# Narrower zero matmuls, masks and selections on GpSimd, and earlier value turns in a fused Sinkhorn attention and maxout kernel

## Chip, cores and metric

The kernel runs on one core of one Trainium2 chip. The metric is the device time of one execution in microseconds (us). In the profile, PE is TensorE's matrix multiplication, PEld its weight load, DVE is VectorE, ACT is ScalarE, POOL is GpSimd and SP is SyncE.

## The reference

Block-sorted attention comes first, and a two-branch maxout layer reads its output. There are 4 batches of 8 heads, 768 positions and head size 64. A sequence has 8 blocks of 96 positions. A small matrix per head (`sort_net`, 8 by 8) goes through five rounds of exponential and of row and column normalisation (Sinkhorn); the result mixes whole blocks of keys and of values. Then each query block attends to its own mixed block.

```python
P = sort_net
for _ in range(5):
    P = P - np.max(P, axis=-1, keepdims=True)
    P = np.exp(P)
    P = P / (np.sum(P, axis=-1, keepdims=True) + 1e-09)
    P = P / (np.sum(P, axis=-2, keepdims=True) + 1e-09)
k_sorted = np.einsum('bhij,bhjcd->bhicd', P, k_b)      # blocks of keys mixed
v_sorted = np.einsum('bhij,bhjcd->bhicd', P, v_b)      # blocks of values mixed
scores = scale * np.matmul(q_b, k_sb.transpose(0, 1, 2, 4, 3))
attn = softmax(scores)                                 # written out in the original
x = np.matmul(attn, v_sb)                              # to 3072 tokens x 512
g = np.maximum(x @ w1, x @ w2)                         # 512 -> 1024
out = g @ w_out                                        # 1024 -> 512
```

Inputs and output are float32; the kernel computes its large products in bfloat16.

## The kernel before

The order of the instructions on each engine is written out by hand (a manual schedule). There are four PSUM buffers of one tag, `ps`, which all TensorE work takes in turn, so a product may have to wait until an earlier one has been copied out. The copies go to ScalarE ("A") or VectorE ("D"), by a letter in the list of steps or by a running count of load (`pick`).

**The opening.** TensorE first runs zero matmuls (`keep_streaming`, with the tile `fill`), 86 of 142 columns, and 12 more of 512 columns: six behind each of two memsets of late weights (`late_zeros`) that stand in rounds 3 and 4 of `sinkhorn`. Meanwhile VectorE and ScalarE run the five rounds of `sinkhorn` on a 32 by 64 tile. In between, `masks` builds `id64`, `maskM` and `maskJ` on VectorE, `selections(0)` builds two selection tiles for batch 0 on VectorE, and ScalarE turns the raw values of batch 0 (`turn_v`, a copy that changes the layout) in four pieces. The last result of the rounds is `p_bf`.

`block_diagonals_first` then expands `p_bf` on TensorE with the constant tiles `one_j` and `sel_v[0]`, and VectorE makes from it the diagonal `bd_k[0]` for the keys, and then `bd_v[0]` for the values. VectorE turns the last piece of the values. Behind it stand two copies that repeat columns of `maskJ` for the later batches; `block_diagonals` (step `pe2`) reads them much later.

**GpSimd** issues the input DMAs, in this order: values of batch 0 (three pieces), keys (three), queries (four). Behind them it builds the selection tiles of batches 1 to 3 (seven copies) and `one_j` (a memset and a copy), and then issues the weights: four DMAs of 256 columns and two of 512 for `w1` and `w2`, then two for `w_out`. Two subtractions (`w_difference`) and the keys of batch 1 follow. A DMA takes the same semaphore as the eighth before it, and waits for that one.

**The front** is a list of steps for batch 0, which begins

```python
front = """
    k0D k1A k2D v1D v2A v3A tq0D v0A tq1D SC1 SC0 F1
    SC2 VA1 SC5 VA0 SC3 F2 VA2 SC4 F0 tx0D SC6 VA3 ...
```

`k` is a third of the key sort with its copy, `v` a quarter of the value sort, `tq` query transposes, `SC` scores with their exponential on ScalarE, `VA` the product with the values and the normalisation on VectorE (a reciprocal and a multiplication), `tx` the transposes of the result, `h` the maxout layer's first product. `k0` begins with zero matmuls, 1024 columns in two of 512. An `F` asks for 512 columns of zeros ahead of the next step.

**The tails.** After the front, each batch's maxout layer is cut into units, and the steps of the next batch's attention stand behind numbered units: `first_tail`, `second_tail`, `third_tail`. `TURN` is `turn_v` on both halves of the values on VectorE, in four pieces of 24 columns. In `second_tail` the pieces stand behind units 8, 9, 11 and 12; the value sorts that read them (`VS`) stand behind 14 and 16. The keys and queries of batch 3 are loaded into the buffer of the raw values, and so behind the turns.

## Time and profile before

| | us |
|---|---|
| median of 4 runs | 167.45 |
| lowest and highest | 167.06 and 167.72 |
| the profiled execution, its own time | 167.49 |
| its span in the profile | 165.7 |
| PE busy in it | 157.9 |
| ACT, DVE, POOL busy | 83.3, 76.5, 32.3 |

The span runs from the first to the last instruction of the program; the rest of the execution's own time lies around it. A row of the timeline has the start, the length, the engine, the line, the operation with output and inputs, and in brackets how long the engine had been idle and what ended that. A row of the chain has start, length and engine. Records of neighbouring instructions of one engine may overlap, since an instruction starts while the one before it is still finishing.

### The profile page before, as it was taken

How to read it: one execution, taken by the hardware profiler on the slowest of the kernel's cores; microseconds unless marked ns; L12 is line 12 of the kernel's file. 1: busy time of each engine (PE TensorE's matmuls, PEld its weight loads, DVE VectorE, ACT ScalarE, POOL GpSimd, SP SyncE). 2: the span in 40 equal slices, each digit the busy share in tenths (PEclk: the TensorE clock that was granted, in tenths of full speed). 3: DMA queues.
4: the chain of work that ended last, by engine and by line, in shares of the span. 5: the costliest groups of instructions: out<-in, count | busy, mean ns of one | idle time of the engine just before them, and what ended most of it. 6: DMA issues, size and time to landing. Idle time of an engine off the chain costs nothing.

```text
span 165.7 us, 4544 instructions
## 1 busy us (share of the span) xinstructions
PE 157.9 (95%) x2000; PEld 96.3 (58%) x2018; DVE 76.5 (46%) x173; ACT 83.3 (50%) x102; POOL 32.3 (19%) x55
## 2 busy tenths in 40 slices
PE   7999899999999999999899999999999999999992
PEld 7948678656555555557555554575655446554451
DVE  4879779465474564615257874250642420000011
ACT  3585985927149845066552253467446306642020
POOL 7998586232013000000004020000000000000000
PEclk9999999999999999999999999999999999999999
DMA  3999999999999996689503999996025294000333
GB/s 51 198 205 197 198 208 205 211 204 223 209 202 213 218 247 70 186 109 188 112 0 62 169 214 179 240 248 39 0 51 174 49 163 142 0 0 0 127 128 129
DMA packets 30404, 23.90 MB, mean 144 GB/s; under 512 B 16752, under 2 KB 25200, under 8 KB 30384
## 3 DMA queue, kind: packets, MB, share of 16 engines
q0 software_dynamic: 11040, 13.37, 47.9%
q1 hardware_dynamic: 19200, 10.17, 28.5%
q8 instruction: 16, 0.26, 0.6%
q10 hardware_dynamic: 144, 0.07, 0.1%
q14 instruction: 4, 0.03, 0.1%
HBM read 26.75 MB, written 6.29 MB: 199 GB/s over the span
## 4 chain that ended last, share of the span: by engine, by line
PE 78%; DVE 9%; DMA 5%; issue 4%; ACT 2%; ACTq 0%
PE out_ps L715 33%; PE h_ps L688 23%; PE o_ps L586 4%; PE wc_ps L668 4%; DMA qT<-q_pair 4%; PE s_ps L559 4%; PE k_ps L469 2%; PE tq_ps L444 2%; ACT e L567 1%; DVE v_dc L257 1%; PE v_ps L534 1%; PE tw_ps L649 1%; PE v_ps L490 1%; DMA p_sb<-in_sort_net_dram 1%; PE tx_ps L624 1%
## 5 line engine op out<-in xcount | busy, mean ns | idle before, releaser
L715 PE MATMUL out_ps<-wo_sb,g 128*128 128x512 bf16 (+2 forms) x187 | 46.0, 370 | 1.4 <-issue 1.0
L688 PE MATMUL h_ps<-xT,w_sb 128*128 128x384 bf16 x256 | 44.5, 326 | 0.0
L688 PEld LDWEIGHTS <-w_sb 128*128 128x128 bf16 x256 | 24.0, 98 | 15.6
L567 ACT ACTIVATE e<-s_ps 96x768 bf16<-96x768 f32 x32 | 23.9, 804 | 13.7 <-PE s_ps L559 13.5
L702 ACT ACTIVATE g<-h_ps 128x768 bf16<-128x768 f32 x27 | 21.8, 811 | 17.8 <-PE h_ps L688 17.7
L715 PEld LDWEIGHTS <-g 128*128 128x128 bf16 x200 | 17.1, 97 | 15.8
L715 PE MATMUL out_ps<-wc,xT 128*128 128x512 bf16 (+2 forms) x98 | 24.7, 370 | 0.1
L108 ACT COPY o<-out_ps 128x1024 f32<-128x1024 f32 x10 | 10.1, 1012 | 28.3 <-PE out_ps L715 25.6
L603 DVE TENSOR_TENSOR x<-o_ps,rs 96x512 bf16<-96x512 f32 x32 | 22.0, 687 | 1.1
L715 PEld LDWEIGHTS <-xT 128*128 128x128 bf16 x100 | 9.6, 97 | 11.2
L586 PEld LDWEIGHTS <-e 96*128 96x128 bf16 x256 | 11.8, 97 | 5.9 <-DVE v_sb L110 0.2
L597 DVE RECIPROCAL rs<-o_ps 96x8 f32<-96x8 f32 x32 | 6.4, 201 | 18.1 <-PE o_ps L586 17.9
L750 DVE COPY o<-out_ps 128x512 f32<-128x512 f32 (+1 forms) x2 | 1.2, 624 | 27.6 <-PE out_ps L715 27.6
L586 PE MATMUL o_ps<-v_sb,e 96*128 96x65 bf16 x256 | 12.9, 193 | 0.0
L110 DVE CAST kT<-k_ps 128x1024 bf16<-128x1024 f32 x7 | 8.3, 1215 | 7.2 <-PE k_ps L469 7.2
L108 ACT CAST v_sb<-v_ps 96x1024 bf16<-96x1024 f32 x10 | 9.8, 1014 | 2.5 <-PE v_ps L490 0.9
L704 DVE TENSOR_SCALAR g<-h_ps 128x768 bf16<-128x768 f32 x5 | 4.8, 956 | 12.2 <-PE h_ps L688 12.2
L559 PE MATMUL s_ps<-qT,kT 64*128 64x96 bf16 x256 | 8.6, 204 | 1.3 <-DMA qT<-q_pair 0.6
L160 POOL DMA_DIRECT2D v_raw<-in_k_dram x3 | 2.5, 823 | 36.8 <-DVE rs L597 36.7
L559 PEld LDWEIGHTS <-kT 64*128 64x128 bf16 x256 | 6.1, 94 | 6.1 <-issue 3.2
L110 DVE CAST v_sb<-v_ps 96x1024 bf16<-96x1024 f32 x6 | 7.3, 1216 | 4.5 <-PE v_ps L534 2.2
L169 POOL DMA_DIRECT2D v_raw<-in_v_dram x11 | 5.9, 543 | 14.4 <-DVE v_dc L257 9.0
(96 smaller groups left out, 144.9 us busy)
## 6 DMA issues: line engine op xcount, KB each, us to landing
out_dram<-o SPq DMA_DIRECT2D x11, 512.0 KB, 3.2
v_raw<-in_v_dram POOLq DMA_DIRECT2D x8, 384.0 KB, 12.4
k_raw<-in_k_dram POOLq DMA_DIRECT2D x9, 256.0 KB, 10.0
w_sb<-in_moe_w_dram POOLq DMA_DIRECT2D x4, 256.0 KB, 7.8
w_sb<-in_moe_w_dram POOLq DMA_DIRECT2D x2, 512.0 KB, 10.9
wo_sb<-in_moe_w_out_dram POOLq DMA_DIRECT2D x2, 512.0 KB, 14.6
v_raw<-in_v_dram POOLq DMA_DIRECT2D x3, 256.0 KB, 4.7
q_raw<-in_q_dram POOLq DMA_DIRECT2D x4, 192.0 KB, 8.7
```

Source lines behind the costliest of these rows:

```text
L108: nc.scalar.copy(out=out_ap, in_=in_ap)
L110: nc.vector.tensor_copy(out=out_ap, in_=in_ap)
L169: nc.gpsimd.dma_start(out=v_raw[r0 : r0 + 64, m * n : (m + 1) * n], in_=v_src[b, :, m * n : (m + 1) * n],)
L559: nc.tensor.matmul(ps[:, h2 * 512 + ii * 128 : h2 * 512 + ii * 128 + BLK], kT[b][rows, (hp * 8 + i) * BLK : (hp * 8 + i) * BLK + 128], rhs ...
L567: nc.scalar.activation(out=e[:, 0 : 8 * BLK].rearrange("p (t c r) -> p t c r", t=8, r=R), in_=ps[0:BLK] .rearrange("p (t f) -> p t f", t=8 ...
L586: nc.tensor.matmul(ps[:, h2 * 512 + ii * 65 : h2 * 512 + (ii + 1) * 65], e[:, (h2 * 4 + ii) * BLK : (h2 * 4 + ii) * BLK + 128], v_sb[:, m0 ...
L597: nc.vector.reciprocal(out=rs, in_=ov[:, :, :, 64])
L603: nc.vector.tensor_tensor(out=x, in0=ov[:, :, :, 0:D], in1=rs.to_broadcast([BLK, 2, 4, D]), op=ALU.mult,)
L668: nc.tensor.matmul(ps[:, 0:512], w2T[:, fb, dmt * 128 : (dmt + 1) * 128], wo_sb[:, fb, :], start=(fb == 0), stop=(fb == NFB - 1),)
L688: nc.tensor.matmul(h_ps[ch, t][:, m * 512 : m * 512 + TCH], w1_sb[:, hp, fb * 128 : (fb + 1) * 128], xT[:, b % 2, ch, hp % 2, hp // 2, :], ...
L702: nc.scalar.activation(out=g, in_=src, func=AF.Relu)
L715: nc.tensor.matmul(dst, g_tiles[b, ch, m // 2][:, m % 2, off : off + 128] if m < NFB else xT[:, b % 2, ch, hp % 2, hp // 2, off : off + 12 ...
```

## The change

The zero matmuls of the opening have 126 columns and not 142, and the two ahead of the first key sort 320 and not 512. The selections of batch 0 and the two copies of `maskJ` are made by GpSimd. In GpSimd's program, `one_j` comes first behind the queries, its memset written as 32-bit words; then the selections of batch 0, the copies of `maskJ`, four weight DMAs, the selections of batches 1 to 3, and the remaining weight DMAs, the subtractions and the keys of batch 1 in the old order. In `second_tail` the four turns stand behind units 6, 8, 9 and 11. The allocations of `id64`, `maskJ` and `maskM` move up in the text. The order of instructions on TensorE, ScalarE and SyncE is the same; VectorE's changes by the four removed copies and by the places of the turns: the first turn comes ahead of one `g` copy of the maxout layer.

```diff
-    for b in range(1, B):
-        selections(b)
     one_j = const.tile([G, 8 * 130], BF16, tag="one_j", name="one_j")
-    nc.gpsimd.memset(one_j, 0.0)
+    nc.gpsimd.memset(one_j.bitcast(U32), 0)
     nc.gpsimd.tensor_copy(
...
-    for t in range(2):
-        load_w_columns(w2_sb, moe_w2, t, t + 1)
-        load_w_columns(w1_sb, moe_w1, t, t + 1)
-    load_w_columns(w2_sb, moe_w2, 2, 4)
-    load_w_columns(w1_sb, moe_w1, 2, 4)
-    load_w(wo_sb, moe_w_out)
+    selections(0)
...
-    w_difference(0, nc.gpsimd)
-    w_difference(1, nc.gpsimd)
-    load_k(1)
...
-        keep_streaming(ps, n)
+        keep_streaming(ps, n, most=320)
...
-    keep_streaming(ps_f32("fill_ps"), 86 * 142, most=142)
+    keep_streaming(ps_f32("fill_ps"), 86 * 126, most=126)
     for it in range(5):
         sinkhorn(it)
         if it < 3:
             masks(it)
         if it == 2:
-            selections(0, nc.vector)
             turn_v(first, "A", 0, 18)
         if it == 3:
             turn_v(first, "A", 18, 36)
+    for c, n, m in [(2, 2, 0), (4, 3, 1)]:
+        nc.gpsimd.tensor_copy(
+            out=maskJ[:, c : c + n],
+            in_=maskJ[:, m].to_broadcast([128, NB, n]).transpose([0, 2, 1]),
+        )
+    for t in range(2):
+        load_w_columns(w2_sb, moe_w2, t, t + 1)
+        load_w_columns(w1_sb, moe_w1, t, t + 1)
+    for b in range(1, B):
+        selections(b)
+    load_w_columns(w2_sb, moe_w2, 2, 4)
+    load_w_columns(w1_sb, moe_w1, 2, 4)
+    load_w(wo_sb, moe_w_out)
+    w_difference(0, nc.gpsimd)
+    w_difference(1, nc.gpsimd)
+    load_k(1)
...
-            sort_k(0, n[0], 1024 if step == front[0] else 0, eng)
+            sort_k(0, n[0], 640 if step == front[0] else 0, eng)
...
-    for c, n, m in [(2, 2, 0), (4, 3, 1)]:
-        nc.vector.tensor_copy(
-            out=maskJ[:, c : c + n],
-            in_=maskJ[:, m].to_broadcast([128, NB, n]).transpose([0, 2, 1]),
-        )
...
-        6: SC[2:4],
+        6: SC[2:4] + [TURN[0]],
         7: [VA[1], TR[0]],
-        8: [VA[2], TURN[0]],
-        9: [VA[3], TR[1], TURN[1]],
+        8: [VA[2], TURN[1]],
+        9: [VA[3], TR[1], TURN[2]],
         10: SC[4:7],
-        11: [VA[4], TURN[2]],
-        12: [VA[5], TR[2], TURN[3], lambda: load_k(3), lambda: load_q(3)],
+        11: [VA[4], TURN[3]],
+        12: [VA[5], TR[2], lambda: load_k(3), lambda: load_q(3)],
```

## The prediction

> **What bounds the kernel now.** I read the page first, then the chain of waits over the whole span, then the timeline of the opening (0 to 25 us), engine by engine, and of the stretch from 78 to 104 us, where the turns are.

> ```profile
> PE 157.9 (95%) x2000; PEld 96.3 (58%) x2018; DVE 76.5 (46%) x173; ACT 83.3 (50%) x102; POOL 32.3 (19%) x55
> ```

> TensorE is busy 95% of 165.7 us, but before 11.3 us that is zeros. So only two things are worth time: the opening, where a serial VectorE chain is waited for, and holes in TensorE's stream later. Of the larger holes behind 19 us (from the start of each matmul to the next, less its columns), one lies where the diff works: 0.41 us at 96.7. Others are 0.46 at 18.4, 0.62 at 19.6 and 0.72 at 78.9.

> The chain in the opening:

> ```profile
> 11.05 0.23 DVE p_bf L285
> 11.32 0.35 PE pe L367 x8
> ...
> 12.62 0.56 DVE v_dc L257
> 13.18 0.43 DVE maskJ L824 x2
> 13.61 0.88 DVE kT L110
> 14.53 1.09 PE v_ps L490 x32
> ...
> 18.07 0.97 DVE qT L110
> 19.08 0.35 PE s_ps L559 x8
> ```

> The five Sinkhorn rounds end in p_bf, TensorE expands it, VectorE makes the diagonals, turns values, copies the masks and empties the first key sort. The value sorts wait for that buffer, and the first scores for the second query transposes. The starts and lengths of the same stretch are in VectorE's timeline:

> ```profile
> 12.54 0.64 DVE L257 COPY v_dc<-v_raw 64x512 uint32<-64x512 uint32 x1
> 13.11 0.49 DVE L824 COPY maskJ<-maskJ 128x16 f32<-128x16 f32 x2
> 13.27 1.20 DVE L110 CAST kT<-k_ps 128x1024 bf16<-128x1024 f32 x1
> ```

> The chain books 0.43 us on the mask copies, because their records end late (13.60). But the key copy starts at 13.27, while they are open, and takes 1.20 us like the next one (14.40, 1.20). What they hold up is start to start: 13.27 - 13.11 = 0.16.

> **The change, part by part.**

> *Selections of batch 0 off VectorE* (two copies, starts 7.79 and 7.89).

> ```profile
> 7.79 0.28 DVE L204 COPY sel_v<-ident 32x64 bf16<-32x64 bf16 x2
> 8.03 0.11 DVE L87 MEMSET late<- 128x64 uint32 x1
> 8.07 0.15 DVE L278 TENSOR_REDUCE rowsum<-p_sb 32x8 f32<-32x64 f32 x1
> ```

> Their 0.24 us looks serial, but the row sum needs ScalarE's exponential, which runs 7.71 to 7.97. In the next round the row sum starts 0.03 behind it (9.79 to 9.83) and takes 0.21. So without the copies it runs 8.00 to 8.21, in place of 8.07 to 8.22: a gain of 0.01. I take 0. The exponential hides these copies.

> *Opening zeros, 86 x 126 columns.* The row of 86 runs 1.20 to 8.58. Starts are 119 ns apart up to 5.2 us and 62 ns after. With 126 columns I estimate 107 ns and 55 ns, from the columns and from L649, whose 128-column transposes go 16 in 0.89 us (56 ns each). So 37 of the wider-spaced ones up to 5.2, then 49 x 0.055 = 2.7, and 0.2 for the last to finish: end near 8.1, 0.5 earlier. The 12 late zero matmuls (0.216 each) follow; the second six wait for a memset at 9.47 behind the fourth round, so they end about 11.0. But TensorE already idles for p_bf (0.15 before 11.32). Worth 0 here; up to 0.5 in an execution whose fast spacing comes later, where the zeros would end after p_bf. Not below 0.

> *Shorter fill at the first key sort.* Two zero matmuls of 512 become 320: 384 columns at 512 in 0.216, 0.16. The first key matmul moves from 12.18 to 12.02; its diagonal ends at 11.97, plus the 0.05 that p_bf to TensorE takes (11.27 to 11.32): it is ready at 12.02 too. ScalarE's copy of the second key sort (13.42, behind TensorE) moves by 0.16.

> *Masks off VectorE*: 0.16 by starts, 0.43 by the chain's ends. I take 0.16. These two edits serve parallel branches (copies on VectorE, matmuls and ScalarE), so together they are 0.16, not 0.32. After them the second value sort waits for the key copy's end, 14.31 in place of 14.47; transposes, their copies (19.03 to 18.87) and ScalarE's eight exponentials, which run without a break from 18.34 to 24.52, follow. The cover for keeping it is DMA slack: GpSimd's weight differences end at 21.16 and 23.81, first read at 23.54 and 25.72, 1.9 us to spare; the values of batches 1 and 2 land by 46.99 and the turn that reads the last of them runs after 48.1.

> *GpSimd's queue.* Before, behind the query issues: seven copies 7.91 to 9.38, a memset of 1.02 to the next start, one copy, then weights from 10.64. After: memset with half the elements (0.5 to 1.0), a copy (0.24), two selections (0.35), two mask copies (0.2 to 0.35 each by the selection rows), so the first weight DMA is issued at 9.4 to 10.2. Four issues at 0.73; the fourth waits for the last key piece (landed 11.64). Then the seven moved copies, 1.47 in all as before, put the fifth weight issue at 13.9 to 14.6, before 14.14. Two more weight issues, two of the output weights, two differences, and the DMAs of the next keys stand behind that. Landings go in order, 17.56, 18.90, 20.27, 21.56, 24.10, with about 10 us between the fifth issue and its landing; that backlog hides the shift, so 0. Without it, up to 0.5 of lateness, inside the 1.9 spare. The first diagonals need the selections by 11.5, and the masks are read at 35.6.

> *GpSimd beside VectorE.* At 9.24 the multiply took 0.26, its peers 0.21, with a GpSimd copy open: 0.05. Copies stay in the rounds, fewer, but now also run from about 12.4, where the diagonal multiply and the turn are. Net 0; bounds from -0.05 to one copy's length, 0.35 lost. [...]

> *Turns one step sooner* (third batch's tail).

> ```profile
> 95.42 0.83 DVE L257 COPY v_dc<-v_raw 128x768 uint32<-128x768 uint32 x1
> 96.17 0.20 DVE L597 RECIPROCAL rs<-o_ps 96x8 f32<-96x8 f32 x1
> 96.40 0.69 DVE L603 TENSOR_TENSOR x<-o_ps,rs 96x512 bf16<-96x512 f32 x1
> ...
> 97.14 0.41 PE L511 MATMUL v_ps<-bd,v_dc 64*128 64x64 bf16 x16 [0.25 <-DVE x L603]
> ```

> The second value sort waits for a buffer freed by a normalisation at 97.08, queued behind the last turn; the matmul before it starts at 96.70 and its like follow each other by 0.03, so 0.41 is lost. That turn moves to 93.83, the others up likewise, and the first goes into a hole, 1.68 us idle before 85.23 for a turn of 0.83. Then the reciprocal starts at 95.42 and the multiply ends near 96.34, before TensorE gets there (96.73): the whole 0.41 goes, with 0.4 to spare, and next late is nothing but TensorE, whose work fills the chain to 162.7. If the hole were closed, the MoE copy at 85.23 would be late by up to 0.83. The key and query loads that wait for the turns go earlier, the first key piece by about 4.5 us, the query by 1.6; they can slow transposes landing at 89.92 and 95.10, first read near 105. The last query transpose pair lands at 111.52 for scores at 114.60. So 0.41, bounds 0 and 0.45.

> Sum: 0.16 + 0.41 = 0.57. The profiled execution took 167.49 (span 165.7): 166.92. The median of 4 is 167.45, so 166.9.

> **The rivals.** *One of the two is given back*, the early 0.16 to GpSimd copies or the late 0.41 to a new wait: 167.04 to 167.29, no change by the bound of 0.3% (0.50 us, about what a measurement of this kernel can tell from none). For it: 0.16 is small beside 0.35. Against: the stretch after 97 is TensorE alone. *More than the sum*: 0.43 at the masks, and late-clock executions lose up to 0.5 less: 166.35 to 166.6. For it: the chain's ends. Against: two key copies of equal length. *Slower*: shorter zeros leave TensorE idle about 0.3 us near 9.4 and 0.3 before 11.3, and matmul spacing doubles again (the page's clock row reads 9 even in the opening; the spacing tells). At the opening the doubled spacing lasted 4.0 us (1.2 to 5.2), in which 2.0 us of work is done, so +2.0 - 0.41 = 169.0. It decides if holes of 0.3 to 0.4 suffice. Against: holes of 0.46 and 0.62 at 18.4 and 19.6 left the spacing unchanged.

> **How the numbers follow.** Forecast 0.46, more 0.10, one given back 0.34, slower 0.10. Range: low 166.35 from the second rival; high 167.5, both gains lost; the clock case is left out. The forecast's own range is 166.7 to 167.05, a little of it above 166.95, so faster 0.53, same 0.37, slower 0.10.

> **What would show it.** Key copy starting near 13.1, first key matmul at 12.0, scores that start at 19.08 near 18.9; p_bf unmoved within 0.05; TensorE idle longer before it; a turn near 83.5 and no hole between the first two value sorts near 96. Wrong: the multiply at 12.4 longer than 0.3, spacing above 62 ns after 9 us, a MoE copy late at 85, or the early shift gone by 25 us.

## The result and the profile after

| | before | after |
|---|---|---|
| median, us | 167.29 (73 runs) | 166.69 (47 runs) |
| profiled execution, us | 167.49 | 166.42 |
| its span, us | 165.7 | 164.6 |

The ratio is 0.9963, with a 95% interval of 0.9951 to 0.9975: 0.62 us faster (0.42 to 0.82). Disturbed executions are left out of the ratio. The profiled pair differs by 1.07, more than the medians; what is known of the extra 0.45 is told below.

The page's first line after:

```profile
PE 157.4 (96%) x2000; PEld 96.1 (58%) x2018; DVE 76.3 (46%) x169; ACT 83.1 (50%) x102; POOL 32.7 (20%) x59
```

VectorE has four instructions fewer and GpSimd four more. The chain of waits in the opening of the kernel after (start, length, engine and line):

```profile
10.86 0.22 DVE p_bf L278
11.08 0.04 issue
11.12 0.35 PE pe L356 x8
...
17.67 0.97 DVE qT L110
18.64 0.04 issue
18.68 0.35 PE s_ps L548 x8
19.03 0.36 PE o_ps L575 x8
19.39 0.83 issue
20.22 0.34 PE s_ps L548 x8
```

Against before, `p_bf`'s expansion is 0.20 sooner (11.32 to 11.12), and the scores that start behind the second query transposes are 0.40 sooner (19.08 to 18.68). Then comes 0.83 of "issue", a wait that no other engine's work ends. The mask copies are gone from VectorE's timeline, and the turn is followed by the key copies at once:

```profile
12.34 0.61 DVE L250 COPY v_dc<-v_raw 64x512 uint32<-64x512 uint32 x1
12.87 2.34 DVE L110 CAST kT<-k_ps 128x1024 bf16<-128x1024 f32 x2
```

The key copy starts 0.40 sooner (13.27 to 12.87). So by 19 us the opening had brought more than the 0.16 that was forecast. One row later, in TensorE's timeline (in brackets the idle time and what ended it), first of after and then of before, it is gone:

```profile
20.22 0.20 PEld L548 LDWEIGHTS <-kT 64*128 64x128 bf16 x8 [0.96 <-issue]
20.22 0.34 PE L548 MATMUL s_ps<-qT,kT 64*128 64x96 bf16 x8 [0.84 <-PE o_ps L575]
```

```profile
20.23 0.20 PEld L559 LDWEIGHTS <-kT 64*128 64x128 bf16 x8 [0.57 <-issue]
20.23 0.34 PE L559 MATMUL s_ps<-qT,kT 64*128 64x96 bf16 x8 [0.45 <-PE o_ps L586]
```

The step SC5 starts at the same time in both, whatever went ahead of it. From there to 79 us the two executions run 0.01 apart. The 1.07 is gained in two places behind. One is the second value sort, where the forecast put it:

```profile
94.77 0.19 DVE L586 RECIPROCAL rs<-o_ps 96x8 f32<-96x8 f32 x1
95.00 0.69 DVE L592 TENSOR_TENSOR x<-o_ps,rs 96x512 bf16<-96x512 f32 x1
95.68 0.34 PE L548 MATMUL s_ps<-qT,kT 64*128 64x96 bf16 x8
95.86 0.63 PE L500 MATMUL v_ps<-bd,v_dc 64*128 64x64 bf16 x32
```

Both sorts now stand in one row of 32 matmuls in 0.63 us; before, the second 16 waited until 97.14 for the normalisation, which now ends at 95.69, ahead of TensorE. That is 0.42. The other is at 79 us, the first scores of batch 2. Before, then after:

```profile
79.80 0.52 PE L559 MATMUL s_ps<-qT,kT 64*128 64x96 bf16 x16 [0.56 <-DMA qT<-q_pair]
```

```profile
79.17 0.51 PE L548 MATMUL s_ps<-qT,kT 64*128 64x96 bf16 x16
```

The query transpose landed 0.89 sooner and a hole of 0.72 is closed: 0.63 more. Between the opening and 79 us the change alters no instruction: the first turn that it moves starts at 82.83, behind this hole.

### The profile page after: what moved, and what is told of

It is laid out like the page before. It is cut to its first block, busy times and chain, and to the rows that moved or that the text cites. A ratio compares the mean times of both kernels' runs of the same rounds, so it can differ in the third digit from the quotient of the medians.

```text
span 164.6 us, 4545 instructions
## 1 busy us (share of the span) xinstructions
PE 157.4 (96%) x2000; PEld 96.1 (58%) x2018; DVE 76.3 (46%) x169; ACT 83.1 (50%) x102; POOL 32.7 (20%) x59
## 4 chain that ended last, share of the span: by engine, by line
PE 88%; DVE 5%; issue 2%; ACT 2%; DMA 1%
PE out_ps L704 37%; PE h_ps L677 26%; PE o_ps L575 5%; PE wc_ps L657 4%; PE k_ps L458 4%; PE s_ps L548 4%; PE tq_ps L433 2%; PE v_ps L479 1%; PE v_ps L523 1%; PE tw_ps L638 1%; ACT e L556 1%; DMA p_sb<-in_sort_net_dram 1%; PE tx_ps L613 1%; DVE colsum L276 1%; DVE p_sb L273 1%
## 5 line engine op out<-in xcount | busy, mean ns | idle before, releaser
L575 PEld LDWEIGHTS <-e 96*128 96x128 bf16 x256 | 11.7, 97 | 5.9 <-DVE v_sb L110 0.2
L110 DVE CAST kT<-k_ps 128x1024 bf16<-128x1024 f32 x7 | 8.3, 1217 | 9.6 <-PE k_ps L458 9.6
L110 DVE CAST v_sb<-v_ps 96x1024 bf16<-96x1024 f32 x6 | 7.3, 1219 | 5.2 <-PE v_ps L523 2.2
## 6 DMA issues: line engine op xcount, KB each, us to landing
wo_sb<-in_moe_w_out_dram POOLq DMA_DIRECT2D x2, 512.0 KB, 14.5
```

The source lines that it names most:

```text
L110: nc.vector.tensor_copy(out=out_ap, in_=in_ap)
L575: nc.tensor.matmul(ps[:, h2 * 512 + ii * 65 : h2 * 512 + (ii + 1) * 65], e[:, (h2 * 4 + ii) * BLK : (h2 * 4 + ii) * BLK + 128], v_sb[:, m0 ...
```

## Experiments

Each is compared with the kernel before in the same runs. The first four: one half of the change each, and the opening's zeros cut in other ways.

**Turns alone**: the kernel before with the four moved turns and nothing else.

```diff
-        6: SC[2:4],
+        6: SC[2:4] + [TURN[0]],
...
-        8: [VA[2], TURN[0]],
-        9: [VA[3], TR[1], TURN[1]],
+        8: [VA[2], TURN[1]],
+        9: [VA[3], TR[1], TURN[2]],
...
-        11: [VA[4], TURN[2]],
-        12: [VA[5], TR[2], TURN[3], lambda: load_k(3), lambda: load_q(3)],
+        11: [VA[4], TURN[3]],
+        12: [VA[5], TR[2], lambda: load_k(3), lambda: load_q(3)],
```

> The kernel before with only the turns of the third batch moved (units 6, 8, 9, 11). Theory: the hole between the first two value sorts near 97 (0.41 us from start to start) is gone and nothing else moves: 0.42 us less, ratio 0.9975. Rival, that the late gain comes from elsewhere in the change: ratio 1.000, hole still there.

Measured: 166.70, ratio 0.9961 (0.9942 to 0.9980), as much as the whole change. TensorE's timeline in it:

```profile
20.51 0.34 PE L559 MATMUL s_ps<-qT,kT 64*128 64x96 bf16 x8 [0.25 <-PE o_ps L586]
```

```profile
79.45 0.52 PE L559 MATMUL s_ps<-qT,kT 64*128 64x96 bf16 x16
```

```profile
96.15 0.63 PE L511 MATMUL v_ps<-bd,v_dc 64*128 64x64 bf16 x32
```

SC5 is even 0.28 later than before, the value sorts have no hole (0.42 gained), and neither have the scores at 79 (0.63 gained).

**Opening alone**: the changed kernel with the turns back in their old places (the same diff, reversed).

> All of the change but the turns. Theory: in both profiles the fifth score step (SC5) starts at 20.22 to 20.23, though all ahead of it is 0.40 us sooner in the changed kernel, so what the opening gains is swallowed there: ratio 1.000 (within 0.001), SC5 again near 20.2, hole near 97 as before. Rival, the prediction's step: the early 0.16 arrives at the end, ratio 0.9990 or, with what the trace shows, 0.9976.

Measured: 167.10, ratio 0.9982 (0.9964 to 1.0000). SC5 starts at 20.24, the scores at 79 wait again (0.64) and so does the second value sort (0.43). A gain of the opening is not told apart from none here, and neither of the two expected ratios is excluded; in the trace none is left at 20.2.

**Half as many zeros of double width** (43 of 252 columns in place of 86 of 126):

```diff
-    keep_streaming(ps_f32("fill_ps"), 86 * 126, most=126)
+    keep_streaming(ps_f32("fill_ps"), 43 * 252, most=252)
```

> The changed kernel, but the opening zeros are 43 matmuls of 252 columns in place of 86 of 126: 86 fewer TensorE instructions ahead of SC5, the same columns. Theory: SC5 waits for the next 16 KB of TensorE's own instructions (packets of kind instruction, at 11.72, 17.74 and 23.84 in the trace, some 250 instructions each), so the end of the stretch that is already there comes 86 instructions later; SC5 starts near 19.4, and up to 0.8 us is kept at the end: ratio to before 0.991 to 0.995. Rival, a wait for data of the kernel: SC5 stays at 20.2, ratio 0.9963 as the changed kernel.

**Late zeros in four times as many pieces** (128 columns in place of 512):

```diff
-            keep_streaming(ps_f32("fill_ps"), 3072, it)
+            keep_streaming(ps_f32("fill_ps"), 3072, it, most=128)
```

> The changed kernel, but the 12 late zero matmuls of 512 columns become 48 of 128: 72 more TensorE instructions ahead of SC5, the same columns, in a stretch where TensorE idles anyway. Theory (instructions arrive late): TensorE runs dry 72 instructions sooner, in the query transposes or first scores near 17, and resumes near 20; 0.5 to 2.5 us longer than the changed kernel. Rival, a wait for data at SC5: within 0.1 us of the changed kernel, SC5 at 20.2.

Measured: 170.53, ratio 1.0213 (1.0175 to 1.0251), and 171.32, ratio 1.0244 (1.0219 to 1.0269). The same zeros cut otherwise cost 3.1 and 3.9 us against the kernel before, 3.8 and 4.6 against the changed one. For 43 zeros both expectations missed: a gain was forecast, or no change. For the small pieces the direction was right, but 0.5 to 2.5 us had been forecast. TensorE's timeline with 43 zeros, and its table of stretches (busy time of PE, PEld, DVE, ACT and POOL with the number of instructions, then PE's granted clock, the DMA share and GB/s):

```profile
18.42 0.85 PE L433 MATMUL tq_ps<-ident,q_raw 128*64 128x128 bf16 x12 [2.41 <-issue]
```

```profile
15.00:20.00 5.00, 2.55 (x52) 2.05 (x47) 2.10 (x3) 1.79 (x2) 3.68 (x5) 0.68 1.45 197
20.00:25.00 5.00, 4.88 (x87) 3.56 (x85) 2.26 (x6) 3.88 (x6) 4.43 (x5) 0.64 1.27 207
```

The clock fell to 0.68 in the 5 us that hold the hole and was 0.64 in the next 5. In stretches of half a microsecond (PE alone) the fall stands inside the hole, which begins at 16.0 (it is 1.00 up to 16.5):

```profile
16.50:17.00 0.50, 0.00 (x0) 0.81 1.41 188
17.00:17.50 0.50, 0.00 (x0) 0.50 1.47 193
```

It stays at 0.50 up to 23.5. TensorE's timeline with the late zeros in small pieces:

```profile
14.13 0.47 PE L458 MATMUL k_ps<-bd,k_raw 64*64 64x64 bf16 x18 [0.81 <-issue]
...
20.43 0.30 PE L433 MATMUL tq_ps<-ident,q_raw 128*64 128x128 bf16 x3 [2.07 <-issue]
```

Holes that "issue" ends again, elsewhere in the program. Counted over the recorded weight loads and matmuls together, they fall at two places: behind number 445 with 43 zeros, behind 447 and 702 with the small pieces, and behind 701 in before, after and the opening alone. The count is of records, and some are missing (the page of after has 2000 matmuls to 2018 weight loads); the expectations call the two places 448 and 704, an estimate of the author's, and so does the table below. In the one run with both holes they are 255 recorded ones apart (447 to 702), some 256 if a record is missing between them. The page of after shows what may come in such portions:

```profile
q8 instruction: 16, 0.26, 0.6%
```

This queue moves 16 packets of 16,384 bytes, and 15 in the kernel with 43 zeros, which has 43 zero matmuls fewer, each with its weight load. That one packet brings TensorE some 256 instructions, what lies between the two places, is an estimate from these numbers; no record names what a packet holds. The first of the 16 starts at 11.72, when TensorE has been at work since 1.2; how the instructions ahead of number 448 came, the trace doesn't show. From the packet records (starts) and TensorE's timeline:

| kernel | packet's start | TensorE goes on | later by |
|---|---|---|---|
| before, behind 704 | 17.74 | 20.23 | 2.49 |
| after, behind 704 | 17.83 | 20.22 | 2.39 |
| turns alone, behind 704 | 18.26 | 20.51 | 2.25 |
| opening alone, behind 704 | 17.71 | 20.24 | 2.53 |
| 43 zeros, behind 448 | 15.95 | 18.42 | 2.47 |
| small pieces, behind 448 | 11.77 | 14.13 | 2.36 |
| small pieces, behind 704 | 17.97 | 20.43 | 2.46 |

The packet for 448 starts near 11.7 in all but the kernel with 43 zeros, and the next follows some 6 us behind, while input data comes in at some 200 GB/s (the last column above). Why the first came 4.2 us later with 43 zeros, and so what asks for a packet, no run shows. So a theory: SC5 waits for TensorE's own instructions, whose packet waits among the input data. It was tested by moving input data without touching TensorE's program.

**Weights later**: GpSimd issues the weights behind a copy that reads the first key copy's result; the first is issued at 14.49 in place of 9.46.

```diff
-    for step in front[:-26]:
+    front_step(front[0])
+    gate = const.tile([32, 2], BF16, tag="gate", name="gate")
+    nc.gpsimd.tensor_copy(out=gate, in_=kT[0][0:32, 0:2])
+    for t in range(2):
+        load_w_columns(w2_sb, moe_w2, t, t + 1)
+        load_w_columns(w1_sb, moe_w1, t, t + 1)
+    load_w_columns(w2_sb, moe_w2, 2, 4)
+    load_w_columns(w1_sb, moe_w1, 2, 4)
+    load_w(wo_sb, moe_w_out)
+    w_difference(0, nc.gpsimd)
+    w_difference(1, nc.gpsimd)
+    load_k(1)
+    for step in front[1:-26]:
```

> The changed kernel, but GpSimd issues the first weight DMA only behind the copy of the first key sort (near 14.2 instead of 9.5). TensorE's instructions come in packets of 256; the packet for instruction 704 starts at 17.8, just as the first weight piece lands, and TensorE stands still for 1.0 us before it. Theory: the packet queues behind data that was issued ahead of it, so without weights queued by 14 it starts near 16.5, instruction 704 is there by 19.2, and 0.5 to 1.0 us less than the changed kernel is left at the end (ratio to before 0.990 to 0.993). Rival: packets come at a pace of about 6 us whatever is queued: start still at 20.2, ratio 0.996 as the changed kernel. Weights that come too late for the first maxout products would show as a hole near 23.

Measured: 167.49, ratio 1.0020 (1.0003 to 1.0037). The packet starts at 15.51 in place of 17.83, SC5 has no hole and starts 0.80 sooner than after. But the weights land too late. GpSimd's and TensorE's rows:

```profile
25.14 2.12 POOL L231 TENSOR_TENSOR w_sb<-w_sb 128x1024 bf16<-128x1024 bf16 x1 [1.80 <-DMA w_sb<-in_moe_w_dram]
```

```profile
27.32 0.50 PE L677 MATMUL h_ps<-xT,w_sb 128*128 128x384 bf16 x2 [1.62 <-POOL w_sb L231]
```

The difference starts 3.2 us later than after's second (21.96), TensorE waits for it, and from there on the execution is 1.62 behind after. So the hole was gone where the packet came sooner, and it came sooner than either expectation had it; the cure cost more than the wait.

**Weights later, old opening**: the same gate on the kernel before with moved turns.

> The opening of the kernel before, with the moved turns, and with the weight DMAs late as in e5. It prices the opening edits where instruction supply does not swallow them: by the prediction 0.16 us longer than e5, by the trace (row sums, fill and masks) 0.2 to 0.35 longer, by the theory that nothing of the opening can arrive 0.0.

Measured: 168.22, ratio 1.0054 (1.0027 to 1.0080). The packet starts at 15.19, and SC5 0.58 sooner than after, so 0.22 later than with the new opening: where the packet is early, the opening edits do reach SC5. The 0.7 between the two times can't be put down to them, since weights land differently and the holes behind them do too (1.33 and 1.11 us here, 0.53 and 1.83 there).

**The first query transpose of batch 2 sooner**: behind unit 18 of the first tail.

```diff
-        18: [VA[2]],
+        18: [VA[2], lambda: q_transposes(2, 0)],
...
-        0: [lambda: q_transposes(2, 0), lambda: q_transposes(2, 1)],
+        0: [lambda: q_transposes(2, 1)],
```

> The changed kernel, but the first query transpose of batch 2 is issued behind unit 18 of the first tail, ten us sooner than before. Theory: the hole of 0 to 0.7 us near 79, which differs from one execution to the next, is always 0, so the median falls by 0.1 to 0.3 us below the changed kernel's and its own spread narrows. Rival: the transposes of the result near 66 to 72 come later by what this one takes, and TensorE waits at 71: up to 1 us longer.

Measured: 166.48, ratio 0.9941 (0.9920 to 0.9963). It is issued at 62.20 in place of 73.23; the scores at 79 have no hole; SC5 is at 20.25.

**Both of these**:

> e5 and e6 together. If both theories hold, their gains add: 0.6 to 1.2 us less than the changed kernel, ratio to before 0.988 to 0.993.

Measured: 167.69, ratio 1.0022 (1.0001 to 1.0043). No hole at SC5 or at 79; the late weights cost 1.03 us at 25.1. So both holes can be closed at once, but the gains did not add as expected: the time is 1.0 us above the changed kernel, and the weights decide.

**A smaller delay of the weights**: the selections of batches 1 to 3 go ahead of the weights, and between them a gate reads `p_bf` (first issue at 11.48). In a second kernel it reads the diagonal of the values, `bd_v[0][0:32, 0:2]` (13.27).

```diff
+    for b in range(1, B):
+        selections(b)
+    gate = const.tile([32, 2], BF16, tag="gate", name="gate")
+    nc.gpsimd.tensor_copy(out=gate, in_=p_bf[:, 0, 0:2])
     for t in range(2):
         load_w_columns(w2_sb, moe_w2, t, t + 1)
         load_w_columns(w1_sb, moe_w1, t, t + 1)
-    for b in range(1, B):
-        selections(b)
```

> The changed kernel with the weight DMAs behind p_bf (first one issued near 11.3; 9.5 in the changed kernel, 14.5 in e5). Theory: the instruction packet asked for near 14.1 waits only for data issued some time before that; with the first weight piece issued 1.8 us later it starts earlier than 17.8, SC5 at 19.4 to 20.0, no hole at 23 to 25, and 0.2 to 0.7 us less than the changed kernel. Rival: what is issued by 14.1 stands ahead of the packet whenever it was issued: start at 17.8, ratio as the changed kernel.

> The same with the weight DMAs behind the value diagonal (first issue near 12.6). Theory: as e9 and more surely, packet start 15.5 to 16.5 as in e5, SC5 at 19.4; the weights land 0 to 1.5 us later than in the changed kernel, against 1.9 us to spare, so the gain of e5 at 22 (0.53 us) is kept to the end: ratio to before 0.992 to 0.995. Rival: the weights come too late as in e5, with holes near 23 and 25: 0.3 to 1 us longer than the changed kernel.

Measured: 166.63, ratio 0.9954 (0.9932 to 0.9977), and 166.44, ratio 0.9942 (0.9922 to 0.9962). With `p_bf` the packet starts at 18.54 and TensorE goes on at 20.95: no help in this execution (167.17, the slowest of its twelve). That the packet is asked for near 14.1 was the author's assumption: in after, TensorE goes past number 445 at 14.16, and no run shows when a packet is asked for. With the diagonal it starts at 17.19, and the hole is gone:

```profile
19.29 0.42 PE L575 MATMUL o_ps<-v_sb,e 96*128 96x65 bf16 x8
19.64 0.34 PE L548 MATMUL s_ps<-qT,kT 64*128 64x96 bf16 x8
```

SC5 is 0.58 sooner than after, although in this execution the scores ahead of it were 0.33 later. Of that, 0.31 is left at 21.4, and nothing from 30 us on (0.15 behind after): the third weight difference, which waits 0.97 for its weights, starts at 28.59 in place of 27.85.

Over all runs, the packet for 704 follows the one before it by 6.0 to 6.6 us where the first weight DMA is issued at 9.4 to 11.5, and by 3.5 to 5.5 where it is issued at 13.0 to 14.7; in that second group TensorE has as many instructions as in before and after, in the same order up to there. That is the evidence for the theory; that the wait is in a queue behind that data is the author's reading of it, and no trace shows where the packet waits.

**The kernel before once more**, to see how far medians wander.

> The kernel before once more, for a second profile: ratio 1.000; the hole near 97 is 0.41 again and SC5 starts at 20.2 to 20.5; the hole near 79 differs from the first profile's 0.72, since it hangs on when a DMA transpose lands.

Measured: 166.92 (12 runs), ratio 0.9983 (0.9966 to 1.0001) against itself. Ratios of single experiments that differ by 0.002 are therefore not told apart. Its profile has the three holes of before: SC5 at 20.25, 0.71 at 79, 0.44 at the value sort.

**The diagonal's gate and the earlier query transpose together**:

> The changed kernel with both edits that helped by themselves: the weight DMAs of the first tail behind the diagonal of the values (first issue about 13.3 us, instruction packet at about 17.2, no hole at TensorE's instruction 704), and the first query transpose of batch 2 one unit sooner (no hole near 79). Theory (the hole near 20 is a late instruction packet, the hole near 79 a late query transpose, and the two are independent): ratio to before about 0.993, 166.1 to 166.4 us; scores of the front's fourth pair start near 19.6, no hole near 79. Rival (the time saved at the opening is given back at the weight differences that land later): as the kernel with the earlier query transpose alone, 166.45 to 166.55, ratio 0.9945 to 0.995.

Measured: 166.26 (12 runs, nine of them from 166.02 to 166.47), the lowest median of all, but the ratio is 0.9944 (0.9924 to 0.9965). The median is the theory's, the ratio the rival's, and its interval holds the changed kernel's ratio too: it is not shown to beat it. The profiled execution (167.39) was the slowest of the twelve. SC5 starts at 19.38, 0.84 sooner than after; then, in VectorE's and TensorE's timelines:

```profile
29.35 0.69 DVE L231 TENSOR_TENSOR w_sb<-w_sb 128x1024 bf16<-128x1024 bf16 x1 [1.98 <-DMA w_sb<-in_moe_w_dram]
```

```profile
30.10 0.82 PE L677 MATMUL h_ps<-xT,w_sb 128*128 128x384 bf16 x4 [0.91 <-DVE w_sb L231]
```

The third weight difference ran 1.50 later than in after (27.85), and from there on the execution is 0.92 behind it.

## Why the prediction was right in its sum and wrong in a part

**Turns, 0.41: right.** Hole gone, 0.42 gained, by the mechanism that was named: the last turn starts at 93.19, the normalisation ends before TensorE gets there. The first turn (82.83 to 83.64) fits into VectorE's gap, and the maxout copy behind it starts at 84.59, on time. The turns alone give as much as the whole measured gain (0.33 to 0.97 us by the interval), and 0.42 of it stands at this place in their trace, which is the main evidence.

**Opening, 0.16: right at the source, wrong at the end.** The shorter fill gave 0.16 (of 0.35 at the first key matmul, 12.18 to 11.83), the masks and the turn ahead of them 0.20 and not the chain's 0.43 (of 0.40 at the key copy): from the start of the turn to the start of the key copy it is 0.53 in place of 0.73, 0.16 forecast and 0.04 by which the turn was shorter. The other 0.20 came with `p_bf`, forecast unmoved: 0.12 of it because the input of `sort_net` landed sooner in this execution (2.39 to 2.27), 0.05 because a multiplication took 0.21 in place of 0.26. All of it ended at 20.2. The step that failed is the one that lets the gain "follow" through transposes and exponentials and looks for its cover in DMA slack. It asked when weights and values land, and never what ended the holes that the prediction itself listed: the 0.62 at 19.6 was taken for a fixed loss that moves along. It was a wait that ended at 20.2 in both, whatever TensorE had done before, and grew to 1.00 when TensorE came 0.40 sooner. The chain of the whole span in before shows it, two rows behind the last one that the prediction prints:

```profile
19.79 0.44 issue
```

TensorE's row at 20.23 has it too, with "0.57 <-issue" in its weight load. The prediction's own sign of being wrong, an early shift that is gone by 25 us, came.

**What took its place.** The ratio gives 0.62, the turns' hole 0.42. That the sum of 0.57 came out so well is in part luck: its 0.16 was lost, and something else that was not forecast made up for it. About 0.2 is left, and in the profiled pair 0.63, all at 79 us. SyncE's rows there, of before and of after:

```profile
73.25 3.54 SPq L430 DMA_TRANSPOSE qT<-q_pair  x1
```

```profile
73.23 2.97 SPq L419 DMA_TRANSPOSE qT<-q_pair  x1
```

Issued at the same time, it took 0.57 longer to issue and landed 6.4 us later in place of 5.5. The three profiles of kernels with the old turns (before, before once more, opening alone) have the slow kind and a hole of 0.64 to 0.72; after, turns alone and the diagonal's gate have the quick kind and none. But with the query transpose moved, the one that stayed (the second of the pair) took 3.74 at 73.20 and landed after 6.6, and there the turns had moved too; and with 43 zeros, also with moved turns, TensorE waited 0.34 for these transposes. Nor can the turns be the cause by order of time, since the first one moved starts at 82.83. It stays open what makes the difference, and whether it is more than the chance of an execution: of the twelve executions of the kernel before once more, eight took 166.60 to 167.01 and four 167.33 to 167.45, the profiled one among the four. That the hole is worth its 0.63 is argued from the profiles; the sooner transpose, which removes it, has a lower median (166.48 against 166.69), but not by more than the intervals allow.

**Costs taken as nothing.** Selections: the row sum of the third round gained 0.01 as worked out. GpSimd's queue: the first weight issue at 9.46 (forecast 9.4 to 10.2), the fifth at 14.23 (13.9 to 14.6). In GpSimd's timeline of after:

```profile
8.78 0.41 POOL L208 COPY sel_v<-ident 32x64 bf16<-32x64 bf16 x2
9.14 0.37 POOL L763 COPY maskJ<-maskJ 128x16 f32<-128x16 f32 x2
9.46 2.23 POOL L189 DMA_DIRECT2D w_sb<-in_moe_w_dram  x3
...
14.23 1.48 POOL L189 DMA_DIRECT2D w_sb<-in_moe_w_dram  x2
```

Contention: the multiplication at 9.10 ran 0.21 us, as its peers, with these copies beside it (one of `sel_v` was open from 8.96 to 9.19), and the diagonal's at 12.20 took 0.22, so not even the 0.05 was lost. The bound of 0.35, the length of one copy, was the author's estimate, and no run shows such a loss: the row at 9.10 lost nothing beside copies; the one at 12.20 stood beside a DMA issue and not a copy, and says nothing on it.

**Opening zeros.** Spacings 106 and 55 ns, as estimated (107 and 55); but the narrow spacing came at 6.1 us and not 5.2, so the row of 86 ended at 8.43, not near 8.1. TensorE's idle time before `p_bf` was 0.09, shorter and not longer as forecast.

**The rivals.** "One of the two given back" did happen, to the early part, though not through GpSimd copies; without the 79 us, the profiled execution would have been 167.05, in its band. "More than the sum" named other sources than the one that came. "Slower" failed by its condition as argued: holes of 1.0 us (after, at 19.2 to 20.2) left the granted clock at 1.00, and so did one of 1.6 to 1.8 (weights later, at 25.5 to 27.3). It isn't empty, though: the kernel with 43 zeros, with a hole of 2.4 to 2.6, had a granted clock of 0.50 up to 23.5.

## What to carry to other kernels

Before a gain is carried along a chain, ask of every hole behind it what ends it: a hole that ends at a fixed time swallows the gain, and only one that is tied to the work ahead of it lets it through. "issue" in front of TensorE, in a stretch where input data comes in (here 0.83 us, at some 200 GB/s), is a suspect: count weight loads and matmuls to it and see whether the holes of two kernels lie a constant number of instructions apart. A change of two parts is best run as its two halves first, since here one half carried the whole sum and the other's gain was visible for nine microseconds and then gone.
